# Attention with routed experts on one core: the value products of a head pair in one run, both heads of a step in one operation, and the slot table behind the first expert tile

## The chip, the cores and the metric

One core of a Trainium2 chip runs the whole program. The metric is the device time of one launch in microseconds. The change is read from the median of several launches; the profile is of one launch.

## What is computed

The reference is causal attention with a decay, a routed layer with eight experts, and a dense layer with a rational activation. Cut to what matters here (4 batches, 8 heads, 576 positions, head size 64; all float32):

```python
scores = q @ k.T / 8 + (cum_i - cum_j)          # cum: running sum of log f
attn = softmax(where(j > i, -1e9, scores))      # rows of 576
x = (attn @ v) as 2304 rows of 512
e = argmax(x @ w_gate)                          # one of 8 experts a row
y = gate * sigmoid * (relu(x @ w1[e]) @ w2[e])  # 512 -> 1024 -> 512
h = y @ w_in                                    # 512 -> 2048
g = (a0 + a1 h + a2 h^2 + a3 h^3) / (1 + |b0||h| + |b1| h^2 + 1e-6)
out = g @ w_out                                 # 2048 -> 512
```

## The kernel before

**Attention.** The loop `pair(p)` takes two heads at a time, 16 pairs for 4 batches. A pair has seven steps: a step is a query tile of 128 rows of one head (i = 0 to 3), the last 64 rows of both heads together (i = 4, "tail"), or, for i = 1 and i = 0, the same tile of both heads as two sets of operations. In a step TensorE makes the scores (`scores`, L444 and L445, two products that together keep float32 accuracy), VectorE adds the mask and finds the row minimum of the negated scores (`least`, L466), ScalarE takes the exponential and the row sum (`weights`, L496), TensorE transposes the weights by blocks of 128 keys (`t2`, L587; `t0` and `t1`, L564 and L568, for the tail), and VectorE or ScalarE copies the transposes from PSUM to the tile pT (`move`, helper lines L280 and L282). Then `pv` (L614) multiplies pT with the values: queries 256 to 575 of both heads are one part, queries 0 to 255 the other. Head 0 fills output rows 0 to 63 and head 1 rows 64 to 127, so these products have the tile shape 128*64 in the profile, where scores and transposes have 128*128. A part is a sum over key blocks j; each j is an operation of its own, and the last block has 64 keys, which makes its shape 64*64. Behind each part an `evac` copies the sum (`ot`). After four pairs `batch(b)` makes the router's logits and the expert choice.

What runs next to what is not in the code's order. Each operation is recorded in a `Plan` with the engines that may take it, their assumed lengths, what it needs, which buffers it takes and frees, and a wished time `when`. `Plan.order` simulates the engines; among operations that could start within NEAR ns of the first it takes the one with the smallest `when`. It decides which engine copies what, too. The wished times are T0 = p * 10000 plus the offsets in the T_ table. PSUM has three banks for scores, three for transposes, two for value products.

**Routing tail.** Behind the last pair, VectorE turns the choices into a table `ids`: which token rows stand in which of 25 slots of 128 rows, each slot of one expert. Then 15 small operations (L1016 to L1030) make `esl`: for each slot whether its expert is new, and the next expert.

**Expert stage.** Weights are split into a high and a low half, `wu[u]` for u = 0 to 3 (two of w1, two of w2). `split_unit(u)` does it in two pieces: ScalarE the high halves, VectorE or GpSimd the low ones (L1060). GpSimd gathers the rows of a slot (`gather`, L1142), TensorE transposes them (`trans_x`, L1161), ScalarE and VectorE make colAh and colAl of them (L1086, L1087), `mm1` (L1167 to L1169) multiplies with w1, `trans_h` (L1182) transposes the result, `mm2` multiplies with w2 into py. In between run `pieces`: the decoding of w_in and w_out for the dense layer, on VectorE, ScalarE and GpSimd's DMA queue. `slot_tokens` and `dense_rows` prepare the dense layer's addresses; `spill` is a flag for rare extra slots. In this stage every engine's order is the code's order.

**Dense stage.** `layer1` and `layer2` over 18 token tiles of 128 rows in five groups (L1374 to L1376, L1419 to L1421).

Of the kernel before, what the change touches and what calls it, by code (L numbers as in the profile page):

```python
# [21 lines left out]
P = 128  # L22
# [15 lines left out]
DEAR = {"ACT": 55.11, "DVE": 322.316}  # L38

NEAR = 106.68  # L40

WARM = 6830


class Op:
    def __init__(self, when, lengths, emit, needs, takes, frees):
        self.when, self.lengths, self.emit = when, lengths, emit
        self.needs, self.takes, self.frees = needs, takes, frees
        self.engine = self.start = self.end = None
# [6 lines left out]
class Plan:  # L56
# [5 lines left out]
    def op(self, when, lengths, emit, needs=(), takes=(), frees=()):  # L62


        o = Op(when, lengths, emit, [n for n in needs if n], list(takes), list(frees))
        self.ops.append(o)
        return o
# [5 lines left out]
    def order(self):  # L73
# [5 lines left out]
        waits = {o: len(o.needs) for o in self.ops}  # L79
        users = {}  # L80
# [5 lines left out]
        def start(o, e):  # L86
            t = max([free.get(e, 0)] + [n.reaches(e) for n in o.needs])
# [8 lines left out]
        while ready:  # L96
# [18 lines left out]
            if e == "PE" and t < WARM:  # L115
                n *= 2
            o.engine, o.start, o.end = e, t, t + n
# [14 lines left out]
def tile_attention_moe_mlp(  # L132
# [81 lines left out]
    with ExitStack() as actx, ExitStack() as rctx:  # L214
# [23 lines left out]

        mask = wk.tile([P, NQ * P], F32, name="mask", bufs=1)
# [14 lines left out]
        NS = len(steps)  # L254

        SPAN = 10000
        T_TRANS = (0.627, 0.134, 0.472, 0.384, 0.239, 0.344, 0.231)
        T_MOVE = (0.739, 0.791, 0.043, -0.438, 0.442, 0.349, 0.365)
        T_LEAST, T_EXP, T_SPLIT, T_SPLIT2 = -0.021, -0.001, 0.692, 0.56
        T_PV, T_PV2, T_PVJ, T_OUT = 1.505, 0.222, 0.046, 0.218  # L260
        T_BATCH, T_BATCHJ, T_ROWS = 0.768, 0.136, 1.212
# [22 lines left out]
        def evac_len(n):  # L284
            return {"ACT": 50 + 0.836 * n, "DVE": 65 + 1.04 * n}
# [64 lines left out]
        def pair(p):  # L350
# [18 lines left out]
            def load_v(e):  # L369
                d["v"] = lt("v", (P, 2, NI, D))  # L370
                nc.sync.dma_start(out=d["v"][:, :, 0:NQ, :], in_=v4[b, hp])
                nc.sync.dma_start(out=d["v"][0:TL, :, NQ, :], in_=vt[b, hp])
# [7 lines left out]
            for h0, h1 in one:  # L380
                n = 820 * (h1 - h0) if p else 1300
# [5 lines left out]
            l_v = plan.op(tl + 0.5 * SPAN, {"SP": 900}, load_v, takes=["v"])  # L387
# [35 lines left out]
            for h in range(2):  # L423
                w = ts + h * T_SPLIT2 * SPAN
                o_kh.append(plan.op(w, {"DVE": 369}, kh(h), [lk[h]] + o_kh[:1], takes=["kh"] if h == 0 else []))
                o_qh.append(plan.op(w + 1, {"ACT": 573}, qh(h), [lq[h]] + o_qh[:1], takes=["q"] if h == 0 else []))
                kle = {"POOL": 1450} if p else {"DVE": 669}
                qle = {"POOL": 1450} if p else {"DVE": 669}
                q2e = {"POOL": 1000} if p else {"DVE": 400}
# [8 lines left out]
            def scores(h, i, u):  # L438
                def go(e):
                    c0 = i * P if h == 0 else S + P + TL + i * P  # L440
                    n = max((i + 1) * P, 256)
                    u["ps"] = bank(ps_s, "s")
                    lhs = d["q"][:, c0 : c0 + P]
                    nc.tensor.matmul(u["ps"][:, :n], lhs, d["kh"][:, h, :n], start=True, stop=False)  # L444
                    nc.tensor.matmul(u["ps"][:, :n], d["q2"][:, c0 : c0 + P], kl_[:, h, :n], start=False, stop=True)  # L445
# [15 lines left out]
            def least(h, i, u):  # L461
                def go(e):
                    w = (i + 1) * P
                    u["t"] = wt("t")
                    u["mn"] = wk.tile([P, 2], F32, tag="mn", name="mn", bufs=8)
                    nc.vector.tensor_tensor_reduce(  # L466
                        out=u["t"][:, :w], in0=u["ps"][:, :w], in1=mask[:, NQ * P - w :], scale=SCALE, scalar=3.0e38,
                        op0=ALU.add, op1=ALU.min, accum_out=u["mn"][:, 0:1],
                    )
# [21 lines left out]
            def weights(h, i, u):  # L491
                def go(e):
# [3 lines left out]
                    nc.scalar.activation(  # L496
# [28 lines left out]
            for si, step in enumerate(steps):  # L525
# [3 lines left out]
                for h, i in step:  # L529
# [9 lines left out]
                    else:  # L539
                        prev, first_e = None, None  # L540
                        oss = []
                        for c in (0, hw):
# [3 lines left out]
                            if c == 0:  # L546
                                first_l = prev
# [958 lines left out]
```

## Time and profile before

| | us |
|---|---|
| time, median of 3 launches (lowest, highest) | 952.83 (952.47, 953.22) |
| time of the profiled launch | 949.95 |
| its span, first to last instruction | 948.1 |
| TensorE busy | 894.9 (94%) |
| VectorE busy | 755.4 (80%) |
| ScalarE busy | 623.7 (66%) |
| GpSimd busy | 347.2 (37%) |

Busy times are of the profiled launch. TensorE's products overlap and their ends are modelled, so how long a product holds the engine is read from the start of it to the start of the next one, not from its own duration.

### The profile page before, as it was taken

What the parts mean: (1) busy time and instruction counts of PE and PEld (TensorE: products, weight loads), DVE (VectorE), ACT (ScalarE), POOL (GpSimd) and SP (SyncE); (2) the same over time, 40 slices, a digit from 0 to 9 for tenths busy, and PEclk for the clock granted to TensorE, in tenths of its full rate; (3) what the DMA queues carried; (4) which work ended last, traced back from release to release, by engine and by line L of the source; (5) the groups of instructions that cost most, each with busy time, mean ns of one, the idle gap of its engine ahead of it and who ended that gap; (6) DMA issues with size and microseconds to landing.
All of it is one profiled execution on the core that took longest, in us unless ns stands there. A gap on an engine that the chain in (4) does not pass through costs nothing. (4 is left out here: it accounts for less than half of the span.)

```text
span 948.1 us, 14923 instructions
## 1 busy us (share of the span) xinstructions
PE 894.9 (94%) x4732; PEld 713.5 (75%) x4733; DVE 755.4 (80%) x1410; ACT 623.7 (66%) x1274; POOL 347.2 (37%) x357
## 2 busy tenths in 40 slices
PE   5999999995589999999999999999999999999996
PEld 5665666563368888888888778889988889988885
DVE  6778888877948668978785499989989878889873
ACT  3787777777036456756653487887777677777664
POOL 7766565624612221312331123243332324223223
PEclk8999999998789999999999999999999999999999
DMA  6754546702455537878864312100100001000001
GB/s 171 168 150 131 157 127 207 210 15 99 138 208 189 194 114 273 298 257 285 287 228 145 135 57 67 34 27 30 34 34 12 23 1 45 24 1 34 1 0 45
DMA packets 50148, 110.26 MB, mean 116 GB/s; under 512 B 8405, under 2 KB 12526, under 8 KB 50062
## 3 DMA queue, kind: packets, MB, share of 16 engines
q1 hardware_dynamic: 39214, 74.09, 25.6%
q0 software_dynamic: 10848, 35.14, 10.8%
q8 instruction: 39, 0.64, 0.3%
q14 instruction: 47, 0.39, 0.1%
HBM read 151.79 MB, written 20.35 MB: 182 GB/s over the span
## 5 line engine op out<-in xcount | busy, mean ns | idle before, releaser
L1405 POOL TENSOR_TENSOR gl<-raw,gh 128x512 fp32r<-128x512 f32 (+1 forms) x80 | 95.4, 1194 | 243.4 <-ACT gh L1404 151.1
L1421 PE MATMUL pa<-wu,gl 128*128 128x512 f32 x288 | 113.0, 392 | 1.1 <-POOL gl L1405 1.1
L1419 PE MATMUL pa<-wu,gh 128*128 128x512 f32 x288 | 113.7, 395 | 0.0
L1420 PE MATMUL pa<-wu,gh 128*128 128x512 f32 x288 | 112.6, 391 | 0.0
L1384 ACT ACTIVATE raw<-ph 128x512 f32<-128x512 f32 (+1 forms) x80 | 44.3, 553 | 79.9 <-PE ph L1376 76.7
L496 ACT ACTIVATE pr<-t,mn 128x384 f32<-128x384 f32 (+3 forms) x128 | 71.1, 557 | 27.6 <-DVE mn L466 25.8
L1087 DVE TENSOR_TENSOR colAl<-px,colAh 128x512 fp32r<-128x512 f32 x70 | 48.0, 687 | 51.4 <-ACTq L1098 28.4
L1060 DVE TENSOR_TENSOR wu<-raw,wu 128x1024 fp32r<-128x1024 f32 x60 | 81.0, 1391 | 7.5 <-ACT wu L1058 7.3
L1387 DVE SCALAR_TENSOR_TENSOR raw<-raw,babs 128x512 f32<-128x512 f32 (+1 forms) x80 | 60.8, 760 | 24.2 <-ACT raw L1385 23.9
L1397 DVE SCALAR_TENSOR_TENSOR raw<-raw,coef,raw 128x512 f32<-128x512 f32 (+1 forms) x80 | 65.9, 824 | 17.6 <-ACT raw L1393 14.5
L1168 PE MATMUL ph<-wu,colAh 128*128 128x512 f32 x176 | 70.7, 402 | 8.2 <-DVE wu L1060 8.2
L1374 PE MATMUL ph<-colAh,wi 128*128 128x512 f32 x192 | 74.9, 390 | 0.8 <-ACTq L1315 0.8
L1375 PE MATMUL ph<-colAl,wi 128*128 128x512 f32 x192 | 74.8, 390 | 0.2 <-DVEq L1315 0.2
L1167 PE MATMUL ph<-wu,colAh 128*128 128x512 f32 x176 | 74.2, 421 | 0.7 <-ACT colAh L1086 0.7
L1376 PE MATMUL ph<-colAh,wi 128*128 128x512 f32 x192 | 74.7, 389 | 0.0
L466 DVE CUSTOM_DVE_ANT_0 t<-s,mask 128x384 f32<-128x384 f32 (+3 forms) x128 | 60.3, 485 | 16.9 <-ACT ot L280 6.9
L1169 PE MATMUL ph<-wu,colAl 128*128 128x512 f32 x176 | 70.7, 402 | 0.0
L1167 PE MATMUL py<-wu,colAh 128*128 128x512 f32 x176 | 70.5, 400 | 0.0
L1169 PE MATMUL py<-wu,colAl 128*128 128x512 f32 x176 | 68.8, 391 | 0.0
L1168 PE MATMUL py<-wu,colAh 128*128 128x512 f32 x176 | 68.7, 390 | 0.0
L614 PE MATMUL po<-pT,v 128*64 128x320 f32 (+4 forms) x448 | 66.4, 380 | 0.4 <-DVE pT L282 0.4
L1086 ACT ACTIVATE colAh<-px 128x512 fp32r<-128x512 f32 x70 | 41.6, 596 | 38.2 <-PE px L1182 25.2
(236 smaller groups left out, 2456.4 us busy)
## 6 DMA issues: line engine op xcount, KB each, us to landing
raw<-in_w_dram SPq DMA_DIRECT2D x92, 1024.0 KB
rk<-in_kT_dram SPq DMA_DIRECT2D x30, 288.0 KB
rq<-in_qT_dram SPq DMA_DIRECT2D x30, 288.0 KB
d<-in_w_in_dram POOLq DMA_DIRECT2D x16, 512.0 KB
d<-in_w_out_dram POOLq DMA_DIRECT2D x16, 512.0 KB
y_d<-ys SPq DMA_DIRECT2D x22, 256.0 KB
v<-in_v_dram SPq DMA_DIRECT2D x16, 256.0 KB
wo_d<-d SPq DMA_DIRECT2D x16, 256.0 KB
```

The source lines that it names most:

```text
L496: nc.scalar.activation(u["pr"][:, :w], u["t"][:, :w], AF.Exp, bias=u["mn"][:, 0:1], scale=-1.0, accum_out=sm[:, i, 2 * hp + h : 2 * hp + h ...
L1060: on.tensor_tensor(w[:, 1], r, w[:, 0].bitcast(F32), ALU.subtract)
L1167: nc.tensor.matmul(ps, hi[:, c, :], w[:, 0, c, :], start=start and c == 0, stop=False)
L1168: nc.tensor.matmul(ps, hi[:, c, :], w[:, 1, c, :], start=False, stop=False)
L1169: nc.tensor.matmul(ps, lo[:, c, :], w[:, 0, c, :], start=False, stop=stop and c == KD - 1)
L1374: nc.tensor.matmul(out_, wh, hi[:, :, c], start=(c == 0), stop=False)
L1375: nc.tensor.matmul(out_, wh, lo[:, :, c], start=False, stop=False)
L1376: nc.tensor.matmul(out_, wl_, hi[:, :, c], start=False, stop=(c == KD - 1))
L1405: nc.gpsimd.tensor_tensor(d["gl"], d["u_"], d["gh"].bitcast(F32), ALU.subtract)
L1419: nc.tensor.matmul(a_, gh[:, sl], wh, start=(m == 0), stop=False)
L1420: nc.tensor.matmul(a_, gh[:, sl], wl_, start=False, stop=False)
L1421: nc.tensor.matmul(a_, gl[:, sl], wh, start=False, stop=(m == MF - 1))
```

## The change

Seven things are changed.

1. In `pv` all key blocks of a part are one operation of the plan, where each block was one. Nothing of another kind can be put between them. The plan knows a `shape` for TensorE's operations and adds SWITCH = 130 ns when it changes.
2. For i = 1 and i = 0 the scores, row minima, exponentials, transposes and copies of both heads are one operation each: the scores of both share a bank, the copy is one instruction.
3. The last key block of the values is 128 deep. The 64 last keys stand in the lower half of the tile, the upper half is zero (three tiles `vs`, set once), and the tail's transposes take the last 128 columns.
4. The T_ table, DEAR, NEAR and the lengths of some operations have other values; the steps have wished times of their own.
5. The 15 operations for `esl` become `slot_info()`, which is called behind `trans_x(0)`.
6. The low halves of wu[1] are made ahead of `trans_x(0)`, and those of wu[2] and wu[3] by VectorE, where GpSimd did it.
7. The load of the spill flag moves to the end of slot 2, `slot_tokens` stands at slot 1 beside `dense_rows`, and the gathers of the token words begin at slot 3.

The diff, cut:

```diff
-NEAR = 106.68
+NEAR = 108.2
+SWITCH = 130
...
-            t = max([free.get(e, 0)] + [n.reaches(e) for n in o.needs])
+            t = free.get(e, 0) + (SWITCH if e == "PE" and o.shape != shape else 0)
+            t = max([t] + [n.reaches(e) for n in o.needs])
...
+        vs = [ld.tile([P, 2, NI, D], F32, name=f"v{i}", bufs=1) for i in range(3)]
+        for t in vs:
+            nc.gpsimd.memset(t[: P - TL, :, NQ], 0.0)
...
-        T_PV, T_PV2, T_PVJ, T_OUT = 1.505, 0.222, 0.046, 0.218
+        T_PV, T_PV2, T_OUT = -2.976, 4.84, -4.781
...
+                    for m, h in enumerate(hs):
+                        c0 = i * P if h == 0 else S + P + TL + i * P
+                        o = u["ps"][:, m * n : (m + 1) * n]
+                        nc.tensor.matmul(o, d["q"][:, c0 : c0 + P], d["kh"][:, h, :n], start=True, stop=False)
+                        nc.tensor.matmul(o, d["q2"][:, c0 : c0 + P], kl_[:, h, :n], start=False, stop=True)
...
-                        nc.tensor.transpose(x["b"][:TL, :P], u["pr"][:, NQ * P : S], identf)
+                        nc.tensor.transpose(x["b"][:, :P], u["pr"][:, S - P : S], identf)
...
-                def pv(j, x=x, part=part, base=base, end=end, last=last):
-                    def go(e):
-                        if j == 0:
-                            x["po"] = bank(ps_o, "po")
-                        kk = P if j < NQ else TL
+                def pv(e, x=x, base=base, end=end, last=last):
+                    x["po"] = bank(ps_o, "po")
+                    for j in range(last + 1):
                         lo = max(base, j * P)
                         for h in range(2):
                             nc.tensor.matmul(
                                 x["po"][h * D : (h + 1) * D, lo - base : end - base],
-                                d["v"][:kk, h, j, :], d["pT"][:kk, h, j, lo:end],
+                                d["v"][:, h, j, :], d["pT"][:, h, j, lo:end],
                                 start=(j == 0), stop=(j == last),
                             )
...
     for u in range(4):
-        split_unit(u, lo=(u == 0))
+        split_unit(u, lo=False)
...
         for s in range(3):
             gather(s)
+        split_unit(0, hi=False)
+        split_unit(1, hi=False)
         trans_x(0, col_of(0))
+        slot_info()
         weights(0, 0)
-        split_unit(1, hi=False)
         weights(1, 0)
-        spill = nc.values_load(esl[NPIPE : NPIPE + 1, 3 : 4], min_val=0, max_val=1)
...
-                split_unit(2, hi=False, on=nc.gpsimd)
+                split_unit(2, hi=False)
...
-                split_unit(3, hi=False, on=nc.gpsimd)
+                split_unit(3, hi=False)
```

What the plan makes of it is seen in the order of the instructions. First TensorE in the second and third pair, before; `po` is a value product, `s` a score, `pt` a transpose.

```order
L614 MATMUL po<-pT,v 64x320 x2
L587 MATMUL pt<-identf,pr 128x128 x4
L444 MATMUL s<-kh,qs_113 128x384
L445 MATMUL s<-kl_119,q2s_117 128x384
L614 MATMUL po<-pT,v 64x320 x2
L587 MATMUL pt<-identf,pr 128x128 x3
L614 MATMUL po<-pT,v 64x192 x2
L614 MATMUL po<-pT,v 64x64 x2
```

One run of value products is cut into single key blocks by transposes and scores of the next pair. The same products of that pair after the change:

```order
L455 MATMUL s<-kh,qs_113 128x256
L456 MATMUL s<-kl_119,q2s_117 128x256
L616 MATMUL po<-pT,v_130 64x320 x6
L616 MATMUL po<-pT,v_130 64x192 x2
L616 MATMUL po<-pT,v_130 64x64 x2
L616 MATMUL po<-pT,v_130 64x256 x2
L616 MATMUL po<-pT,v_130 64x128 x2
L573 MATMUL pt<-identf,pr 128x128 x4
```

Both parts of the pair now stand together, seven key blocks with two heads each. Up to the last of them, 92 such runs stand in TensorE's order before, and 16 after.

The second place is VectorE behind the routing tail (`esl` and `info` belong to the slot operations, `wu` to the splits, `colAl` to the token tiles). Before:

```order
L1028 TENSOR_SCALAR esl<-en 25x1
L1029 SCALAR_TENSOR_TENSOR esl<-en,chg 25x1
L1030 CAST esl<-usd 25x1
L1060 TENSOR_TENSOR wu_3514<-raw_82,wu_3514 128x1024 x2
L1087 TENSOR_TENSOR colAl<-px,colAh 128x512
L1060 TENSOR_TENSOR wu_3515<-raw_83,wu_3515 128x1024 x2
L1263 TENSOR_LOAD esl
L1087 TENSOR_TENSOR colAl<-px,colAh 128x512
```

After the change, from the ids on:

```order
L1007 TENSOR_SCALAR ids<-pid 128x25
L1037 TENSOR_TENSOR wu_3323<-raw_82,wu_3323 128x1024 x2
L1037 TENSOR_TENSOR wu_3324<-raw_83,wu_3324 128x1024 x2
L1064 TENSOR_TENSOR colAl<-px,colAh 128x512
L1112 TENSOR_SCALAR info<-send_3241,pcol 25x9
```

The splits of wu[0] and wu[1] stand ahead of the first token tile, and the slot operations behind it. Further on in the same order, after the change, the splits that GpSimd made before:

```order
L1209 TENSOR_SCALAR d_3487<-d_3483 128x512
L1211 SCALAR_TENSOR_TENSOR d_3487<-d_3483,d_3487 128x512
L1037 TENSOR_TENSOR wu_3325<-raw_84,wu_3325 128x1024 x2
L1213 SCALAR_TENSOR_TENSOR d_3487<-d_3483,d_3487 128x512
L1216 SCALAR_TENSOR_TENSOR d_3487<-da,d_3487 128x512
L1075 COMPARE_AND_BRANCH
L1037 TENSOR_TENSOR wu_3324<-raw_83,wu_3324 128x1024 x2
L1075 UNCONDITIONAL_BRANCH x2
L1223 TENSOR_TENSOR wi_3327<-d_3487,wi_3327 128x512
L1064 TENSOR_TENSOR colAl<-px,colAh 128x512
L1037 TENSOR_TENSOR wu_3326<-raw_85,wu_3326 128x1024 x2
```

wu[2] and wu[3] (the numbers 3325 and 3326) stand among the decoding steps; the split between the two branches is skipped while the expert stays the same.

## Rows read from the trace of the kernel before

**Rows 1.** Busy time by stretch (us from the span's start), instructions, clock, DMA

```profile
core 0: us, PE busy (x) PEld busy (x) DVE busy (x) ACT busy (x) POOL busy (x), PEclk, DMA share, GB/s
13.49:219.23 205.74, 194.45 (x1344) 128.34 (x1344) 163.69 (x544) 153.49 (x478) 118.49 (x126) 0.99 0.55 146
...
240.04:272.45 32.41, 19.44 (x67) 13.20 (x66) 23.22 (x31) 5.20 (x10) 15.99 (x12) 0.72 0.55 187
272.45:948.10 675.65, 665.96 (x3163) 559.87 (x3161) 542.05 (x775) 446.97 (x760) 190.56 (x180) 1.00 0.31 104
```

**Rows 2.** Timeline of TensorE in attention: start, us, engine, line, operation

```profile
130.40 0.66 PE L587 MATMUL pt<-identf,pr 128*128 128x128 f32 x4
130.98 0.76 PE L614 MATMUL po<-pT,v 128*64 128x320 f32 x4
131.67 0.44 PE L444 MATMUL s<-kh,qs 128*128 128x384 f32 x1
...
132.22 0.76 PE L614 MATMUL po<-pT,v 128*64 128x320 f32 x4
...
133.39 0.81 PE L614 MATMUL po<-pT,v 128*64 128x192 f32 x8
134.12 0.39 PE L444 MATMUL s<-kh,qs 128*128 128x256 f32 x1
```

**Rows 3.** Timeline of TensorE in the first pairs

```profile
28.42 1.30 PE L614 MATMUL po<-pT,v 128*64 128x320 f32 x8
29.65 0.40 PE L455 MATMUL s<-kh,qs 128*128 128x288 f32 x1
...
31.71 0.34 PE L444 MATMUL s<-kh,qs 128*128 128x384 f32 x1
...
32.06 0.49 PE L587 MATMUL pt<-identf,pr 128*128 128x128 f32 x3
```

**Rows 4.** Timeline of TensorE, transposes in a row in the last pair

```profile
214.16 1.04 PE L587 MATMUL pt<-identf,pr 128*128 128x128 f32 x8
215.03 0.60 PE L779 MATMUL pt<-identf,ot 128*128 128x128 f32 x4
```

**Rows 5.** Timeline of VectorE at the expert stage's start; idle before in brackets

```profile
240.15 0.21 DVE L1016 TENSOR_SCALAR eq<-send,pcol 25x9 f32<-25x9 f32 x1
...
242.13 2.34 DVE L1060 TENSOR_TENSOR wu<-raw,wu 128x1024 fp32r<-128x1024 f32 x2
245.42 0.69 DVE L1087 TENSOR_TENSOR colAl<-px,colAh 128x512 fp32r<-128x512 f32 x1 [0.95 <-ACT colAh L1086]
246.03 12.63 DVE L1060 TENSOR_TENSOR wu<-raw,wu 128x1024 fp32r<-128x1024 f32 x2
```

**Rows 6.** Timeline of GpSimd in the same stretch

```profile
241.91 0.97 POOL L1142 DMA_INDIRECT xg<-x_d,ids  x1 [0.30 <-issue]
...
247.11 9.32 POOL L1060 TENSOR_TENSOR wu<-raw,wu 128x1024 fp32r<-128x1024 f32 x4
```

**Rows 7.** Timeline of TensorE there

```profile
257.58 0.80 PE L1168 MATMUL ph<-wu,colAh 128*128 128x512 f32 x1 [8.16 <-DVE wu L1060]
...
266.44 0.38 PE L1132 MATMUL px<-identf,ids_t 128*25 128x128 f32 x1 [3.90 <-DVE ids_t L1130]
...
272.45 0.48 PE L1167 MATMUL py<-wu,colAh 128*128 128x512 f32 x1
```

**Rows 8.** Busy time in four us there, columns as in rows 1

```profile
256.00:260.00 4.00, 2.42 (x6) 1.93 (x7) 3.82 (x5) 0.00 (x0) 0.44 (x1) 0.50 0.11 9
```

**Rows 9.** VectorE's copies in attention by shape: count, busy us, mean ns, idle before

```profile
L282 DVE COPY pT<-pt 128x512 f32<-128x512 f32 x14 | 9.4, 674 | 4.2 <-PE pt L587 4.2
...
L282 DVE COPY pT<-pt 128x128 f32<-128x128 f32 x16 | 4.3, 280 | 0.0
...
L282 DVE COPY pT<-pt 128x256 f32<-128x256 f32 x7 | 2.7, 395 | 0.4 <-PE pt L587 0.4
```

**Rows 10.** Timeline of ScalarE at the first block of w_in

```profile
252.51 0.66 ACT L1206 ACTIVATE da<-d 128x512 f32<-128x512 f32 x1 [2.64 <-DMA d<-in_w_in_dram]
```

**Rows 11.** TensorE's waits in attention: total us, times, longest us

```profile
PE s L444 <- DVE mn L466: 4.4, 6, 1.1
```

More of the change, by code (lines that the diff above doesn't have):

```diff
@@ L34, with __init__ @@
 }
-DEAR = {"ACT": 55.11, "DVE": 322.316}
-NEAR = 106.68
+DEAR = {"ACT": 45.9, "DVE": 316.0}
+NEAR = 108.2
 WARM = 6830
+SWITCH = 130
 class Op:
-    def __init__(self, when, lengths, emit, needs, takes, frees):
-        self.when, self.lengths, self.emit = when, lengths, emit
+    def __init__(self, when, lengths, emit, needs, takes, frees, shape):
+        self.when, self.lengths, self.emit, self.shape = when, lengths, emit, shape
         self.needs, self.takes, self.frees = needs, takes, frees
@@ L60, in __init__, with op @@
         self.buffers, self.ops = buffers, []
-    def op(self, when, lengths, emit, needs=(), takes=(), frees=()):
-        o = Op(when, lengths, emit, [n for n in needs if n], list(takes), list(frees))
+    def op(self, when, lengths, emit, needs=(), takes=(), frees=(), shape=0):
+        o = Op(when, lengths, emit, [n for n in needs if n], list(takes), list(frees), shape)
         self.ops.append(o)
@@ L79, in order @@
         waits = {o: len(o.needs) for o in self.ops}
+        shape = 0
         users = {}
@@ L116, in order @@
                 n *= 2
+            if e == "PE":
+                shape = o.shape
             o.engine, o.start, o.end = e, t, t + n
@@ L615, in go @@
                                 x["po"][h * D : (h + 1) * D, lo - base : end - base],
-                                d["v"][:kk, h, j, :], d["pT"][:kk, h, j, lo:end],
+                                d["v"][:, h, j, :], d["pT"][:, h, j, lo:end],
                                 start=(j == 0), stop=(j == last),
                             )
-                    return go
-                prev = first = None
-                for j in range(last + 1):
-                    lo = max(base, j * P)
-                    prev = plan.op(wP + dP * j, {"PE": (end - lo) * 4 / 2.4 + 58}, pv(j), (o_pv_need[part] if j == 0 else []) + [prev, l_v],
-                                   takes=[] if j else ["po"], frees=[("pT", pt_first[0]), ("v", l_v)] if j == last else [])
-                    first = first or prev
+                n_cols = sum(end - max(base, j * P) for j in range(last + 1))
+                first = prev = plan.op(
+                    wP, {"PE": n_cols * 4 / 2.4}, pv, o_pv_need[part] + [l_v], takes=["po"],
+                    frees=[("pT", pt_first[0]), ("v", l_v)], shape=1,
+                )
                 def out_t(e, x=x, base=base, end=end):
```

199 lines of the change are left out of this document (95 added, 104 removed).

## The prediction

> **What bounds the kernel now.** I read the busy times by stretch first [rows 1]. Three of the stages matter: attention (13.49 to 219.23 us), the start of the expert stage (240.04 to 272.45, behind the routing tail), and the rest. In attention TensorE is busy 194.45 of 205.74 us, 94.5%; VectorE 163.69 (80%), ScalarE 153.49 (75%). So TensorE is the bound, and VectorE is not far behind. In the expert start nothing is full: TensorE 19.44 and VectorE 23.22 of 32.41 us. From 272.45 on TensorE is full, 665.96 of 675.65. So time saved ahead of 272.45 moves the end by as much, unless a new wait appears behind it.
>
> Next, how TensorE fills attention. Its timeline shows the products with the values (L614, 64 output columns a head, so shape 128*64) as single key blocks between transposes and scores (128*128) [rows 2]. A lone 320-column block holds the engine from 130.98 to 131.67, 0.69 us. Two blocks in a row take 1.23 us (28.42 to 29.65) [rows 3], so a block is worth 1.23 - 0.69 = 0.54, and 0.15 is lost in each run. The neighbours lose as well: four transposes between two such runs take 0.58 (130.40 to 130.98) against 4 x 0.109 = 0.44 (eight take 0.87, 214.16 to 215.03 [rows 4]); a pair of 384-column scores takes 0.55 (131.67 to 132.22) against 0.35 (31.71 to 32.06 [rows 3]). So one run costs 0.15 + 0.14 = 0.29 beside transposes and 0.15 + 0.20 = 0.35 beside scores.
>
> Then the expert start. The VectorE timeline has the slot operations from 240.15 to 242.13, then the low halves of wu[0], two pieces in 2.34 us, so 1.17 each, then those of wu[1], two pieces in 12.63 us [rows 5]. In those microseconds GpSimd ran its four pieces for wu[2] and wu[3], 247.11 to 256.43 [rows 6]: VectorE's second piece came out only after GpSimd was through. TensorE sat 8.16 us for it, sat 3.90 us more for the token ids queued on VectorE, and began mm2 of slot 0 at 272.45 [rows 7]; behind the first wait it came back at the lower clock, 1.2 GHz (0.50 granted [rows 8]).
>
> **The change part by part.** *Runs of the value products.* Counted in the order of TensorE's instructions, 92 runs become 16: one per pair, both parts together. 76 runs at 0.29 to 0.35, middle 0.32, are 24.3 us. In addition the 64-row block of the last keys becomes 128 rows deep: today its run (192 and 64 columns, 133.39 to 134.12 [rows 2]) takes 0.73, where 256 columns at 0.54 / 320 are 0.43 and the run loses 0.15, so 0.15 is left for this inner change of shape; 16 times, 2.4. The extra 64 key rows cost nothing: the column count is the same, and the zeros are set once by three small memsets, under the loads that the first scores wait for. TensorE's need falls by 26.7, to 167.8 us.
>
> *Both heads in one operation.* Per pair two 256-column and two 128-column copies become one of 512 and one of 256. On VectorE that is 2 x 395 + 2 x 280 = 1350 ns against 674 + 395 = 1069 [rows 9]; 16 pairs give 4.5 us, and I take ScalarE's price for the same. By the counts in the order the new table takes 19 copies off VectorE (92 become 73) and 13 off ScalarE (116 become 103), wide ones and narrow ones exchanged, so the most comes off VectorE: about 4 and 1. Needs: VectorE 159.5, ScalarE 152.5.
>
> *What attention then takes.* TensorE at today's 94.5% would need 177.5 us: 28 saved. The other end: VectorE at today's 80% needs 200 us: 5 saved. Between them I take TensorE at 90%, 186 us, VectorE at 86%: **20 saved**. It is nearer the first end since TensorE still needs most. What speaks for a loss of share is the run of 3 us itself (1600 columns at 0.54 / 320, plus its edges), in which no score and no transpose is made. VectorE then lives on at most three score banks, some 1.6 us at the price of like-sized copies (0.40 to 0.67 [rows 9]), and on the transposes waiting. It may starve for 1 us a pair; with 186 us it has (186 - 159.5) / 16 = 1.7 us a pair to spare, so this is covered, barely.
>
> *Expert start.* The two pieces for wu[1] go ahead of the first colAl, those for wu[2] and wu[3] leave GpSimd, and the slot operations stand behind colAl. VectorE: ids at 240.15, four pieces of 1.17 until 244.8, still ahead of colAl at 245.42, which waits for ScalarE [rows 5]. So mm1 of slot 0 starts as now. The slot operations then take 2.0 until 248.1; they delay only the weight loads on SP, whose targets are wanted some 20 us later. The half product mm1(0,1) runs on at 257.58 - 8.16 = 249.4. The next that is late is mm2(0,0), which needs the transposed h of slot 0. By the new VectorE order, each step at the price of colAl's 0.69 if it is as wide: second colAl until about 250.7, two decode steps at most 1.4, wu[2] 2.34, two decode steps 1.4, about 0.9 for ScalarE's answer, 0.69 for wi, 0.69 for colAl: 258.1. TensorE has the rest of mm1(0,1), mm1(1,0) and three sets of four transposes to do, 35 instructions at the 0.21 us that one takes in the full stretch (665.96 / 3163 [rows 1]): 7.4, until 256.8. So it waits over 1 us there. 272.45 - 258.1 = 14.3 saved, if the first w_in block has landed by 250.7. Now ScalarE waited for it until 252.51 [rows 10], behind weight loads that will start later; if it is no earlier, 12.5. **I take 14.** The spill flag's register load, formerly ahead of mm1(0,0) on every engine, moves to slot 2; I cost it at nothing, since TensorE waited for colAh there. Token ids and dense rows, now together at slot 1, are some 1.5 us of VectorE in a stage where TensorE is the bound. The routing tail keeps its operations: 0, give or take 1.
>
> The sum: -20 - 14 = -34 against this execution's 949.95 us (span 948.1 and 1.85 around it), 916. The median of the runs shown is 2.9 above it, so the time as measured should be **919 us**.
>
> **A page beside the rows.** The Trainium skill, "TensorEngine Tiling (Array Packing)", PSUM Bottleneck, says that tiling makes TensorE faster but not the copies out of PSUM, which may then become the limit. By it the copies, VectorE's above all, would set attention, and the time would be that of rival 1. No run here shows it yet.
>
> **The rivals.** *1. VectorE or the bursts set attention.* VectorE gets no busier than today's 80%: 5 saved there, 14 at the expert start: 934 us. For it: VectorE at 159.5 and TensorE at 167.8 are near each other, and the runs of 3 us. Against it: VectorE idles 42 us now, with a TensorE that is full. 0.20.
>
> *2. The first gathers are held.* GpSimd issues them as soon as the ids are there, now while VectorE runs four split pieces. If GpSimd has to let all pass, 4 x 1.17 = 4.7 us are lost: 924 us. Against it: the gather at 241.91 took 0.97 [rows 6], with VectorE's pieces from 242.13 on [rows 5]. 0.07. The Trainium skill, "SBUF — State Buffer", SBUF: two separate sides, gives VectorE and GpSimd a port pair that one of them holds for its whole instruction, and warns that descriptor writing on GpSimd can be locked out by it. The trace shows the lock between operations with two inputs on both engines (the 12.63 us), and not with this gather.
>
> *3. TensorE keeps its 94.5%.* 28 + 14 saved: 911 us. 0.07.
>
> *4. Slower.* A whole run waits for its last copy from PSUM, and all later scores and transposes of TensorE stand behind it; before, single blocks slipped between. TensorE at 90% already idles 186 - 167.8 = 18 us, 1.1 a pair; it decides from 34 / 16 = 2.1 us a pair more, 3.2 in all. Against it: TensorE's waits on VectorE's row minima come to 4.4 us in attention, the longest 1.1 [rows 11], and in the new order scores of another pair mostly stand between a pair's last transposes and its run. 0.03, about 960 us.
>
> *5. The attention part gives nothing* (the new order loses what the runs save): 14 alone, 939 us. 0.03.
>
> **How the numbers follow.** The forecast has 0.60, its own range 912 to 926 (attention 15 to 25, expert start 11 to 15). The range that holds 8 in 10 reaches over rivals 2 and 3 and most of rival 1: 907 to 935. A measurement of this kernel can tell 0.2%, 1.9 us, from no change. Rival 4 ends slower; in 0.02 I expect the sum to come to nothing. That is 0.95 faster, 0.02 the same, 0.03 slower.
>
> **What would show it.** Right: the value products in 16 runs of about 3 us; attention at 181 to 191 us with TensorE busy near 168; pieces of 1.2 us for all of wu on VectorE, no wait of 8.16 us, a granted clock of 1.00 from the first mm1 on, mm2 of slot 0 some 18 us after the ids. Wrong: TensorE waits of over 1.5 us a pair for copies into pT or row minima (rival 1 or 4), a first gathered tile transposed later than 4 us after the ids (rival 2), or new waits of TensorE behind the expert start.

## Result and the profile after

The changed kernel takes **915.87 us** (median of 4 runs, 915.42 to 916.76) against 952.65 for the kernel before in the same session: ratio 0.9617, 95% interval 0.9601 to 0.9634. The profiled execution took 916.76 us, its span 915.0 (before 949.95 and 948.1).

The stretches of the kernel after, with TensorE (PE), its weight loads, VectorE (DVE), ScalarE (ACT) and GpSimd (POOL) busy in us, the granted clock, the share of the DMA engines and GB/s. They answer to [rows 1] and [rows 8]:

```profile
core 0: us, PE busy (x) PEld busy (x) DVE busy (x) ACT busy (x) POOL busy (x), PEclk, DMA share, GB/s
13.52:192.90 179.38, 167.24 (x1340) 135.94 (x1340) 155.53 (x525) 148.00 (x464) 118.56 (x127) 0.98 0.62 167
192.90:214.00 21.10, 8.63 (x87) 6.41 (x87) 17.08 (x48) 14.50 (x23) 10.87 (x11) 0.79 0.32 113
214.00:232.05 18.05, 15.50 (x66) 9.95 (x65) 13.20 (x28) 4.14 (x8) 8.05 (x8) 0.86 0.69 231
214.00:915.00 701.00, 685.18 (x3227) 570.63 (x3225) 560.02 (x810) 452.43 (x768) 197.78 (x188) 0.99 0.32 109
246.00:250.00 4.00, 4.00 (x13) 3.05 (x13) 0.88 (x4) 0.09 (x1) 0.00 (x0) 0.57 0.41 137
```

Attention fell from 205.74 to 179.38 us, the routing tail went from 20.81 to 21.10, and the part from the ids to the end fell from 708.06 to 701.00: -26.4 + 0.3 - 7.1 = -33.2, the spans' difference of 33.1.

TensorE's timeline after (start, time, line and operation, in brackets the idle time before and what ended it), answering to [rows 2, 7]:

```profile
189.95 3.02 PE L616 MATMUL po<-pT,v 128*64 128x320 f32 x28
218.83 0.66 PE L1163 MATMUL px<-identf,xg 128*128 128x128 f32 x4 [0.60 <-DMA xg<-x_d,ids]
232.05 0.50 PE L1169 MATMUL py<-wu,colAh 128*128 128x512 f32 x1 [1.27 <-ACT colAh L1063]
245.26 0.27 PE L1134 MATMUL px<-identf,ids_t 128*25 128x128 f32 x1 [3.21 <-DVE ids_t L1132]
250.07 0.48 PE L1169 MATMUL py<-wu,colAh 128*128 128x512 f32 x1
```

The 28 products of a pair are now one run of 3.02 us. In the expert stage mm2(s,k) is half k (0 or 1) of slot s's product with w2. mm2(0,0) starts 18.05 us behind the ids (32.41 before), with no wait of 8 us ahead of it. But slot 1 stops for the transposed token ids, 3.21 us, and the products behind that wait run at a granted clock of 0.57, so mm2(1,0) stands 250.07 - 214.00 = 36.07 us behind the ids. Before it was 284.76 - 240.04 = 44.72:

```profile
284.76 0.48 PE L1167 MATMUL py<-wu,colAh 128*128 128x512 f32 x1
```

VectorE and GpSimd there, answering to [rows 5] and [rows 6]:

```profile
214.00 0.19 DVE L1007 TENSOR_SCALAR ids<-pid 128x25 int32<-128x25 f32 x1 [0.40 <-PE pid L1005]
214.31 4.63 DVE L1037 TENSOR_TENSOR wu<-raw,wu 128x1024 fp32r<-128x1024 f32 x4
220.77 0.38 DVE L1112 TENSOR_SCALAR info<-send,pcol 25x9 f32<-25x9 f32 x1
244.33 0.69 DVE L1216 SCALAR_TENSOR_TENSOR d<-da,d 128x512 f32<-128x512 f32 x1
244.94 0.17 DVE L1132 CAST ids_t<-ids 128x25 f32<-128x25 int32 x1
```

```profile
214.48 2.00 POOL L1144 DMA_INDIRECT xg<-x_d,ids  x1 [4.70 <-DVE ids L1007]
216.79 1.86 POOL L1144 DMA_INDIRECT xg<-x_d,ids  x1 [0.31 <-issue]
218.96 0.95 POOL L1144 DMA_INDIRECT xg<-x_d,ids  x1 [0.30 <-DMA xg<-x_d,ids]
```

Four low halves take 4.63 us, 1.16 each. The cast of the ids is a 0.17 us step that stands behind VectorE's whole list for the slot. The first two gathers, beside the four pieces, took about twice the 0.97 of [rows 6] and the 1.08 of the first one before:

```profile
240.52 1.08 POOL L1142 DMA_INDIRECT xg<-x_d,ids  x1 [4.70 <-DVE eq L1016]
```

TensorE's waits from 40 to 190 us (us in all, times, longest), to be set beside [rows 11]:

```profile
PE s L466 <- DVE mn L478: 4.8, 2, 2.6
PE pt L713 <- ACT lgs L705: 1.4, 1, 1.4
PE pt L593 <- DVE pT L292: 0.7, 1, 0.7
```

### The profile page after: what moved, and what is told of

It reads as the page before. It is cut to its first block, busy times and chain, and to the rows that moved or that the text cites. A ratio compares the mean times of both kernels' runs of the same rounds, so it can differ in the third digit from the quotient of the medians.

```text
span 915.0 us, 14857 instructions
## 1 busy us (share of the span) xinstructions
PE 868.4 (95%) x4733; PEld 720.1 (79%) x4733; DVE 742.2 (81%) x1395; ACT 619.1 (68%) x1261; POOL 339.6 (37%) x356
## 3 DMA queue, kind: packets, MB, share of 16 engines
q1 hardware_dynamic: 39214, 74.09, 26.4%
q0 software_dynamic: 10848, 35.14, 11.3%
## 5 line engine op out<-in xcount | busy, mean ns | idle before, releaser
L1037 DVE TENSOR_TENSOR wu<-raw,wu 128x1024 fp32r<-128x1024 f32 x64 | 75.4, 1221 | 8.4 <-ACT wu L1035 8.0
L510 ACT ACTIVATE pr<-t,mn 128x384 f32<-128x384 f32 (+3 forms) x128 | 70.6, 555 | 16.1 <-DVE mn L478 15.6
L1401 DVE SCALAR_TENSOR_TENSOR raw<-raw,coef,raw 128x512 f32<-128x512 f32 (+1 forms) x80 | 66.0, 825 | 17.4 <-ACT raw L1397 14.4
L1063 ACT ACTIVATE colAh<-px 128x512 fp32r<-128x512 f32 x70 | 41.6, 596 | 37.4 <-PE px L1184 26.1
L1035 ACT ACTIVATE wu<-raw 128x1024 fp32r<-128x1024 f32 x64 | 63.8, 1053 | 3.2 <-DMA raw<-in_w_dram 2.8
L1425 PEld LDWEIGHTS pa<-wu,gl 128*128 128x128 f32 x288 | 54.0, 188 | 14.0 <-POOL gl L1409 2.4
```

Source lines behind the costliest of these rows:

```text
L510: nc.scalar.activation(u["pr"][:, sl], u["t"][:, sl], AF.Exp, bias=u["mn"][:, m : m + 1], scale=-1.0, accum_out=sm[:, i, 2 * hp + h : 2 * ...
L1037: nc.vector.tensor_tensor(w[:, 1], r, w[:, 0].bitcast(F32), ALU.subtract)
L1425: nc.tensor.matmul(a_, gl[:, sl], wh, start=False, stop=(m == MF - 1))
```

## The experiments

My theory had two parts. In attention, TensorE loses time each time it changes the shape of its matmuls, so grouping gains what the changes cost. In the expert start, GpSimd's splits held VectorE up (below: the lock), and that wait is gone. The rivals: the gain of attention comes from the merged heads and new due times (the wished times of the plan); the expert start is worth nothing, or hangs on the order of VectorE's list rather than on GpSimd. All ratios are to the kernel before; the change stands at 0.9617.

How much one profiled execution can tell: five kernels with the change's attention took 179.38 to 181.51 us in it, five with the old one 205.74 to 210.11. From the ids to the end, kernels that differ only in attention from the change took 700.38 to 702.16.

### Attention: one part undone, or one part alone

**The products apart.** The changed kernel with one planned operation for each key block again, and a rule that keeps like shapes apart:

```diff
-            t = free.get(e, 0) + (SWITCH if e == "PE" and o.shape != shape else 0)
+            t = free.get(e, 0) + (200 if e == "PE" and o.shape == shape == 1 else 0)
...
-                first = prev = plan.op(
-                    wP, {"PE": n_cols * 4 / 2.4}, pv, o_pv_need[part] + [l_v], takes=["po"],
+                for j in range(last + 1):
+                    n_cols = end - max(base, j * P)
+                    prev = plan.op(wP, {"PE": n_cols * 4 / 2.4}, pv(j), ...
```

> This is the changed kernel in which a query part's value products are one planned operation for each key block again, and the plan is told to keep same-shaped operations apart: the products stand in 103 runs between other shapes instead of 16; the heads stay merged and the expert start stays as changed. My theory, that entering and leaving the value products' tile shape costs TensorE time (0.29 to 0.35 us for a run): 87 more runs by 0.32 are 28 us more of TensorE, and the attention is 20 to 28 us longer than the 179.4 us of the change, total 935 to 944 us. Rival: the attention's gain came from the merged heads' fewer copies and the new table of due times; then this kernel is within 5 us of the change (915 to 921 us).

Measured: 947.82 us, ratio 0.9949 (0.9932 to 0.9965), above the theory's 935 to 944. Its attention:

```profile
13.56:225.20 211.64, 200.68 (x1348) 133.72 (x1350) 159.14 (x527) 150.37 (x462) 120.49 (x130) 0.98 0.53 142
```

32.3 us longer than in the change, TensorE's busy time 33.4 more: 0.37 to 0.38 us for each of 87 runs, a little over the price that I took, and attention is more than the expected 20 to 28 us longer. The rival falls: merged heads and new due times without the grouping are not faster in attention than the kernel before. The due times were made for grouped products, though, so this run doesn't show what merged heads are worth with a table made for products apart.

**The last key block over 64 rows again.**

```diff
+                        kk = P if j < NQ else TL
-                                d["v"][:, h, j, :], d["pT"][:, h, j, lo:end],
+                                d["v"][:kk, h, j, :], d["pT"][:kk, h, j, lo:end],
...
-                        nc.tensor.transpose(x["b"][:, :P], u["pr"][:, S - P : S], identf)
+                        nc.tensor.transpose(x["b"][:TL, :P], u["pr"][:, NQ * P : S], identf)
```

> This is the changed kernel with the last key block's value products over 64 rows as before, not 128 rows with zeros in half of them. The prediction priced the shape change inside a run at 0.15 us for each of the 16 products of that block, 2.4 us of TensorE. By the prediction: 2 to 3 us slower than the change (918 to 919 us), with TensorE's busy time in the attention 2.4 us up. Rival: in the trace of the change a step from another shape costs only as much as the shape behind it makes it, and the last product of a run leaves for scores or transposes in either case: within 0.7 us of the change (915.2 to 916.6 us).

Measured: 922.18 us, ratio 0.9681 (0.9655 to 0.9708). Attention and one run:

```profile
13.41:197.76 184.35, 173.36 (x1341) 137.13 (x1341) 154.74 (x525) 148.72 (x464) 118.87 (x126) 0.97 0.62 162
...
194.51 3.32 PE L617 MATMUL po<-pT,v 128*64 128x320 f32 x28
```

Neither number: attention is 5.0 us longer and TensorE 6.1 us busier, where the prediction had 2.4. One run shows why for most of it: 3.32 against 3.02 us, 0.30 for each of 16 runs, 4.8 in all. The 64-column block stands inside the run, ahead of the 256-column block of the second part, so its shape is entered and left; the prediction had counted 0.15. The 1.3 us of busy time that are left are not the block's for certain: behind a wait of 1.96 us for row minima this trace has a short stretch at half clock (granted 0.50, so 1.2 GHz), in which the same products take longer. The trace of the change has none in attention after 40 us, though it waits 2.21 us at the same place; the products apart and the merged products alone have one too, near 101 us.

```profile
103.00:106.00 3.00, 3.00 (x17) 3.00 (x15) 2.10 (x8) 2.46 (x8) 1.20 (x2) 0.50 0.03 5
```

**The heads apart.** The changed kernel with every (head, block) a step of its own, the due times of a pair written twice:

```diff
-        steps = [[(0, 2)], [(0, 3)], [(0, NQ)], [(1, 3)], [(1, 2)], [(0, 1), (1, 1)], [(0, 0), (1, 0)]]
+        steps = [[(0, 2)], [(0, 3)], [(0, NQ)], [(1, 3)], [(1, 2)], [(0, 1)], [(1, 1)], [(0, 0)], [(1, 0)]]
```

> This is the changed kernel with the steps of the two heads as operations of their own again, each with the due time that the pair had: the value products stand in 32 runs instead of 16, and the small copies of the first two query blocks are twice as many. My theory: 16 more runs by 0.32 us are 5 us more of TensorE, the copies 4 to 5 us more of VectorE and ScalarE together, so 4 to 8 us more than the change (920 to 924 us). Rival A (VectorE is close behind TensorE and now sets the end): 8 us or more (924 and up). Rival B (only the value products' grouping counts, and runs of the small parts are hidden): under 2 us more (916 to 918 us).

Measured: 933.58 us, ratio 0.9801 (0.9768 to 0.9835), by its profile 14.7 us more in attention and tail together. Rival A's number, but not its reason:

```profile
13.54:211.49 197.95, 182.83 (x1377) 143.57 (x1377) 157.79 (x524) 159.37 (x513) 123.18 (x132) 0.98 0.59 156
211.49:228.74 17.25, 4.90 (x49) 3.21 (x49) 14.11 (x39) 10.97 (x16) 5.74 (x6) 0.68 0.25 83
...
PE pt L593 <- DVE pT L292: 4.2, 2, 2.2
```

VectorE is at 80% there and ScalarE at 81%, TensorE at 92%; TensorE's own busy time rose most, by 15.6 us, of which 16 more runs at 0.32 explain 5. What makes up the rest isn't shown; the next run bears on it.

**The products merged, nothing else**, on the kernel before with its own due times:

```diff
-                    prev = plan.op(wP + dP * j, {"PE": (end - lo) * 4 / 2.4 + 58}, pv(j), (o_pv_need[part] if j == 0 else []) + [prev, l_v],
+                first = prev = plan.op(
+                    wP, {"PE": n_cols * 4 / 2.4 + 58}, pv, o_pv_need[part] + [l_v], takes=["po"],
```

> This is the kernel before with its value products merged into one planned operation for each query part, and nothing else changed (heads apart, the last key block over 64 rows, the old expert start and the old due times): 32 runs instead of 92. By the price of 0.29 to 0.35 us for a run, 60 runs are 19 us of TensorE; at the share that TensorE then held the attention goes from 205.7 to 186 to 191 us, the time is 14 to 20 us under before (933 to 939 us). Rival (from the run with the heads apart, which was 16 us slower than the change): the grouping alone starves VectorE and ScalarE, and without merged heads and fitted due times only 5 to 10 us are saved (943 to 948 us).

Measured: 938.56 us, ratio 0.9865 (0.9846 to 0.9885), 13.1 us under before in the same session. The time is inside the theory's 933 to 939 us and the saving just short of its 14 to 20; attention, at 193.04, is above its 186 to 191. The rival's 5 to 10 us fall.

```profile
13.61:206.65 193.04, 180.37 (x1362) 137.10 (x1362) 153.12 (x534) 154.94 (x492) 120.19 (x127) 0.98 0.60 156
206.65:225.16 18.51, 6.48 (x64) 4.60 (x64) 17.07 (x49) 12.62 (x19) 8.68 (x9) 0.69 0.33 115
...
PE pt L587 <- DVE pT L282: 6.3, 3, 3.0
```

The kernel before has this wait for copies too, in the same window of 40 to 190 us:

```profile
PE pt L587 <- DVE pT L282: 3.2, 2, 1.6
```

Attention and tail together are 211.55 us here, 226.55 before, 200.48 in the change, 215.20 with the heads apart. So grouping alone, at 32 runs, gives 15.0 of the 26.1 us, with 3.1 us more of waits for copies; merged heads, the 128-row block and the new table give the other 11.1, and some 4.8 of these are the block (above). The kernel with the heads apart has this grouping and the block, and is still 3.7 us slower than grouping alone. So something else in it costs time, and its 14.7 us are no price of the heads; the table of due times, made for merged heads, is the likeliest, but no run shows it. Merged heads and table can't be told apart by these runs.

One count goes with most of this. I went through TensorE's records in attention and counted where a matmul has other row or column counts than the one ahead of it: 231 changes before, 44 in the change, 99, 140 and 222 in the kernels with 64 rows, with merged products alone and with products apart. Busy time above the change's, divided by the changes more: 27.2 / 187 = 0.146, 6.1 / 55 = 0.11, 13.1 / 96 = 0.14, 33.4 / 178 = 0.19 us for each. With the heads apart the count fails: 85 changes, 15.6 / 41 = 0.38, or 11.9 / 34 = 0.35 with the tail, of which this kernel does 3.7 us of TensorE's work earlier. So changes of shape are not all that makes TensorE busier there, and the price of one is known only as a range.

### The expert start

Eight kernels run here change it. The table gives, from each trace, the us from the start of the ids on VectorE to mm2(0,0), to mm2(1,0), and to the end of the span.

| kernel | mm2(0,0) | mm2(1,0) | end |
|---|---|---|---|
| before | 32.41 | 44.72 | 708.06 |
| before, low halves on VectorE | 28.59 | 40.92 | 704.58 |
| before, tokens at slot 1 | 25.94 | 43.24 | 707.47 |
| before, both of these | 18.50 | 37.27 | 701.41 |
| before, the whole new start | 18.80 | 37.59 | 701.93 |
| after | 18.05 | 36.07 | 701.00 |
| after, two low halves on GpSimd | 25.47 | 44.04 | 709.12 |
| after, gathers first | 18.54 | 36.36 | 701.72 |
| after, ids early | 17.72 | 30.69 | 696.01 |
| after, ids early and gathers first | 18.00 | 32.38 | 697.68 |

**The new start on the kernel before**, the attention as it was (the hunks from `slot_info` on, as in the diff of the change):

> This is the kernel before with the expert-start part of the change alone (all four low halves on VectorE, gathers issued earlier, the facts of the slots worked out later); the attention stays as it was, with its 92 runs of value products. My theory from the trace of the change: mm2(0,0) comes about 14 us nearer to the token ids, but the wait for the transposed ids (3.2 us) and the lower clock behind it give some 5.7 us back before slot 1, and the later slots about 1 more, so that 7 to 9 us of the time before are saved (944 to 946 us) and mm2(1,0) comes 8.7 us nearer to the ids. Rival A: the start is worth its full 14 us when the attention in front of it is unchanged (939 us). Rival B: the start is worth nothing, and all 37 us come from the attention (952 us).

Measured: 945.66 us, ratio 0.993 (0.9904 to 0.9957), 4 to 9 us saved. The time and mm2(0,0), 13.6 us nearer to the ids, are as the theory had them. mm2(1,0) came 7.1 us nearer for an expected 8.7, and ids to end gained 6.1 us for an expected 7 to 9. Both rivals are out.

**Only the low halves moved to VectorE:**

```diff
-                split_unit(2, hi=False, on=nc.gpsimd)
+                split_unit(2, hi=False)
...
-                split_unit(3, hi=False, on=nc.gpsimd)
+                split_unit(3, hi=False)
```

> This is the kernel before with one thing changed: the low halves of the third and fourth expert unit are subtracted on VectorE instead of GpSimd, in the same places of the program. My theory (GpSimd's split and VectorE's held each other up in the kernel before): VectorE's pieces there fall from 12.63 to about 2.4 us, TensorE's wait of 8.16 us in front of mm2(0,0) is gone, and most of the 14 us that the start gained in the change are seen already, so 5 to 10 us less than before (943 to 948 us). Rival: the wait is one for VectorE's place in line, not for the shared port; the four GpSimd pieces then only move to VectorE, and the time is within 2 us of before (951 to 955 us).

Measured: 948.23 us, ratio 0.995 (0.9932 to 0.9968): 3 to 6.5 us saved, 3.5 from ids to end, at or under the low end of the theory's 5 to 10. The rival's time is out, but what it says of VectorE's line holds in part: the lock is gone, and the wait is not.

```profile
254.33 2.35 DVE L1060 TENSOR_TENSOR wu<-raw,wu 128x1024 fp32r<-128x1024 f32 x2
260.05 2.35 DVE L1060 TENSOR_TENSOR wu<-raw,wu 128x1024 fp32r<-128x1024 f32 x2
263.38 0.17 DVE L1130 CAST ids_t<-ids 128x25 f32<-128x25 int32 x1
...
263.70 0.38 PE L1132 MATMUL px<-identf,ids_t 128*25 128x128 f32 x1 [11.31 <-DVE ids_t L1130]
```

Every piece takes 1.2 us now. Before, the piece that the lock held was the first of wu[1]'s two, not the second, as the prediction reads it:

```profile
246.03 11.50 DVE L1060 TENSOR_TENSOR wu<-raw,wu 128x1024 fp32r<-128x1024 f32 x1
```

In this run TensorE sits 11.31 us for a 0.17 us cast that is queued on VectorE behind these pieces and the decode steps.

**Only the token ids moved, from slot 0 to slot 1:**

```diff
-            if s == 0:
-                slot_tokens()
             if s == 1:
+                slot_tokens()
                 dense_rows()
```

> This is the kernel before with the cast and transpose of the token ids moved from slot 0 to slot 1, and nothing else changed; GpSimd still splits two units. By the prediction the 8.16 us wait stays and only the 3.90 us wait for the ids leaves the front of mm2(0,0): mm2(0,0) about 28 us after the ids instead of 32.4, the time 1 to 4 us under before (949 to 952 us). Rival: the place of the token ids in VectorE's line is what sets mm2(0,0), and the splits on GpSimd only fill the wait: mm2(0,0) at 18 to 22 us, 8 us or more under before.

Measured: 950.61 us, ratio 0.9992 (0.9973 to 1.001), no change that can be told. mm2(0,0) came 6.5 us earlier, between the theory's 28 us and the rival's 18 to 22, and mm2(1,0) 1.5: the wait had only moved one slot on.

```profile
257.62 0.80 PE L1168 MATMUL ph<-wu,colAh 128*128 128x512 f32 x1 [8.18 <-DVE wu L1060]
265.97 0.47 PE L1167 MATMUL py<-wu,colAh 128*128 128x512 f32 x1
278.51 0.38 PE L1132 MATMUL px<-identf,ids_t 128*25 128x128 f32 x1 [3.21 <-DVE ids_t L1130]
```

**Both of these moves:**

> This is the kernel before with two things changed at once: the low halves of the third and fourth unit on VectorE, and the token ids moved to slot 1. Alone the first brought mm2(0,0) from 32.4 to 28.6 us after the ids, with an 11.31 us wait for the token ids in front. If these two are the whole of the expert start: mm2(0,0) at 18 to 20 us and the time 6 to 9 us under before (944 to 947 us), as in the run with all of the start's changes. Rival: the earlier split of the second unit and the later slot facts matter as well: mm2(0,0) at 22 us or later, under 5 us saved (above 948 us).

Measured: 946.09 us, ratio 0.9934 (0.9915 to 0.9953). mm2(0,0) at 18.50 us: these two edits are the whole expert start. Alone they brought 3.8 and 6.5 us at mm2(0,0), together 13.9. The earlier second split and the later slot facts add nothing that is seen (18.80 us with the whole new start).

**The two low halves back on GpSimd**, in the changed kernel:

```diff
-                split_unit(2, hi=False)
+                split_unit(2, hi=False, on=nc.gpsimd)
...
-                split_unit(3, hi=False)
+                split_unit(3, hi=False, on=nc.gpsimd)
```

> This is the changed kernel with the low halves of the third and fourth unit back on GpSimd, as before the change; all else as changed. By the prediction (VectorE's and GpSimd's two-input operations hold each other up): VectorE's operations between 220 and 232 us (colAl, the decode steps) grow, mm2(0,0) comes 3 to 8 us later after the ids than the 18.05 us of the change, and the time is 3 to 8 us over the change (919 to 924 us). Rival: what VectorE runs there now, behind the split of the second unit, doesn't collide, and the split is off its queue: mm2(0,0) within 1 us of 18 us or earlier, the time within 1.5 us of the change.

Measured: 925.19 us, ratio 0.9709 (0.9686 to 0.9732), 8.8 us over the change by the ratios, 8.1 by the table, so a little above the theory's 3 to 8. mm2(0,0) came 7.4 us later, and the rival falls. The lock is back, in another place than I had named. GpSimd, VectorE, TensorE:

```profile
223.85 9.37 POOL L1037 TENSOR_TENSOR wu<-raw,wu 128x1024 fp32r<-128x1024 f32 x4
...
222.32 10.93 DVE L1112 TENSOR_SCALAR info<-send,pcol 25x9 f32<-25x9 f32 x1
...
235.91 0.80 PE L1169 MATMUL ph<-wu,colAh 128*128 128x512 f32 x1 [5.86 <-ACTq L1075]
```

The same operation on 25 x 9 numbers takes 0.38 us in the change. Here it came out at 233.25, when GpSimd's pieces ended (233.22), and all of VectorE stood behind it. It had begun 1.5 us ahead of the pieces' first record; what held it in that time isn't shown.

### What the change left behind

**The token ids early:** cast ahead of the first split, transposed behind the first gathered rows at slot 0.

```diff
+        slot_cast()
         split_unit(0, hi=False)
...
+                if s == 0:
+                    slot_tokens()
...
             if s == 1:
-                slot_tokens()
                 dense_rows()
```

> This is the changed kernel with the token ids cast before the first split and transposed behind the first rows at slot 0, not at slot 1 behind VectorE's work. My theory: the 3.21 us that TensorE waits for the cast ids and the lower clock of the products behind it (granted 0.57 in that stretch) are what the start gives back, so mm2(1,0) comes about 5 us nearer to the ids and the time is 4 to 5.5 us under the change (910.4 to 911.9 us). Rival A: the wait moves to VectorE's next late piece (the copies and splits behind), 0 to 1.5 us gained (914.4 to 916). Rival B: the clock falls at this place whatever is waited for: only the wait itself is gained, 3 us (912.5 to 913).

Measured: 912.59 us, ratio **0.9568** (0.9544 to 0.9593), faster than the change with intervals that don't touch, by 4.7 us by the ratios. The median itself is where rival B had it (912.5 to 913), but its reason is out, since the clock didn't fall. From ids to end 5.0 us less, and mm2(1,0) 5.4 us nearer, as the theory had it; its profiled attention was 2.1 us longer, within the spread above. The ids wait for nothing, and the stretch that ran at 0.57 has the full clock:

```profile
225.35 0.27 PE L1139 MATMUL px<-identf,ids_t 128*25 128x128 f32 x1
246.98 0.48 PE L1174 MATMUL py<-wu,colAh 128*128 128x512 f32 x1
...
246.00:250.00 4.00, 4.00 (x22) 3.25 (x21) 3.55 (x9) 3.15 (x5) 2.13 (x3) 1.00 0.54 172
```

**The gathers first:** slot facts, first split, first tile, second split.

```diff
+        slot_info()
         split_unit(0, hi=False)
-        split_unit(1, hi=False)
         trans_x(0, col_of(0))
-        slot_info()
+        split_unit(1, hi=False)
```

> This is the changed kernel with the second unit's low half and the facts of the slots exchanged around the first gathered tile (facts, first split, first tile, second split). My theory: the first gathers took 2.0 and 1.9 us because VectorE's split ran beside their issue; the first split still does, so at most the later tile gains, and the second split now stands behind the first tile's own split on VectorE: within 1 us of the change (915 to 916.5 us). Rival: the gathers fall to about 1.0 us and the first tile is transposed 0.8 us earlier, and all of it reaches the end: 1 to 2 us faster (914 to 915 us).

Measured: 917.52 us, ratio 0.963 (0.9606 to 0.9654), the change's time within the intervals, though the median is 1 us above the expected range. The gathers are short again and the first tile is transposed 4.03 us behind the ids instead of 4.83, but mm2(0,0) is no earlier:

```profile
214.46 1.07 POOL L1144 DMA_INDIRECT xg<-x_d,ids  x1 [4.70 <-DVE info L1112]
217.11 1.05 POOL L1144 DMA_INDIRECT xg<-x_d,ids  x1 [0.30 <-issue]
...
226.49 0.43 DVE L1209 TENSOR_SCALAR d<-d 128x512 uint32<-128x512 uint32 x1 [2.05 <-DMA d<-in_w_in_dram]
...
232.52 0.50 PE L1169 MATMUL py<-wu,colAh 128*128 128x512 f32 x1 [2.65 <-ACT colAh L1063]
```

VectorE waits 2.05 us for the w_in block, which lands no earlier, and mm2(0,0) hangs on what follows from it. The change waits 0.70 us for that block (below). The rival falls.

**Both edits:**

> The two last kernels' edits together. If both are independent: the sum of their gains, 4 to 6.5 us under the change (909.5 to 912 us). Rival: the ids stand in the way of the first split, so less than the better of the two alone (above 912 us).

Measured: 913.28 us, ratio 0.9581 (0.9557 to 0.9604), not told apart from the ids alone. That is the rival's number (above 912), but no run shows its reason. The early ids are the best version found.

## Why the prediction was right, and where its steps were not

The time was 915.87, predicted 919; the profiled execution 916.76, the sum 916. That is closer than the steps were, and luck: attention's saving was put 6 us too small and the expert start's 7 us too large, both outside the ranges that the prediction gave them (15 to 25 and 11 to 15), and the two errors cancelled. The two mechanisms, fewer runs and no split on GpSimd, are borne out.

- *Runs of the value products.* TensorE's need of 167.8 us is measured as 167.24. Inside this sum errors cancel, too. The 64-row block was undersized (some 4.8 for 2.4). Restoring the runs cost more than the priced 0.32 (0.37 us each). Removing 60 of them alone gave less: 14.1 us of TensorE's busy time, 0.23 each, and 12.7 us of attention. Merging the heads was put at nothing on TensorE; with the heads apart it is 15.6 us busier, more than the runs explain.
- *"Between them I take TensorE at 90%, 186 us."* This step failed: TensorE held 93.2%, so 26.4 us were saved, not 20. I had feared that a run of 3 us starves VectorE and that TensorE pays for it afterwards. It idled 12.1 us in attention, not 18, little more than the 11.3 before; its named waits from 40 to 190 us come to 8.4, most of it two waits for row minima. VectorE, at 155.53 us for a forecast 159.5, stands at 87%. With heads apart and the old table the fear comes true in a small part (6.3 us of waits for copies, where the kernel before has 3.2).
- *The page on tiling.* By what the Trainium skill, "TensorEngine Tiling (Array Packing)", PSUM Bottleneck, says, that the copies may become the limit, VectorE would have set attention. The trace doesn't bear that out for the whole change: TensorE at 93% still sets it.
- *Expert start, at mm2(0,0).* Right to 0.1 us: 18.05 us behind the ids, forecast 258.1 - 240.04 = 18.06. That it is so close is luck: the first w_in block came 12.0 us behind the ids, not by the assumed 10.7, and the chain of VectorE that the forecast adds up ended with colAl at 18.89. But mm2(0,0) begins with products that need colAh only, and just its third one waits for colAl (rows below). The reason was half the story. Four splits on GpSimd are a real lock, shown both ways, but with the ids left in VectorE's list at slot 0 taking it away gives 3.8 us, not 14.
- *"Token ids and dense rows, now together at slot 1, are some 1.5 us of VectorE in a stage where TensorE is the bound."* This step failed. At slot 1 TensorE was waiting for VectorE's list: 3.21 us, and slower products behind it. 14.4 us at mm2(0,0) were 8.7 at mm2(1,0) and 7.1 at the end, not 14. The forecast of a full clock from the first mm1 on was wrong for the same reason. The early ids give 5.0 us of it back.
- *From mm2(1,0) on* the change takes 664.93 us and before 663.34. Across all kernels run here this stretch took 663.3 to 665.4, with before the shortest, so whether these 1.6 us come from the change or are scatter stays open.
- *Rivals.* 1, 4 and 5 didn't come. 3 nearly came in attention: 26.4 of its 28 us, with TensorE's share at 93.2% for its 94.5%; the forecast had given it 0.07. 2 came in part (two gathers held, the first tile at 4.83 us, past the 4 us that the prediction named as its sign) and cost next to nothing, since VectorE waits for the w_in block behind it.

The rows after the change on which the reading of mm2(0,0) rests, VectorE's and TensorE's:

```profile
226.03 0.43 DVE L1209 TENSOR_SCALAR d<-d 128x512 uint32<-128x512 uint32 x1 [0.70 <-DMA d<-in_w_in_dram]
...
232.21 0.68 DVE L1064 TENSOR_TENSOR colAl<-px,colAh 128x512 fp32r<-128x512 f32 x1
...
232.95 0.50 PE L1171 MATMUL py<-wu,colAl 128*128 128x512 f32 x1 [0.17 <-DVE colAl L1064]
```

## What to carry to other kernels

Where TensorE is the bound, count how often neighbouring matmuls change shape, inside a planned operation too; here each change was worth 0.11 to 0.19 us of its busy time in four comparisons, and a fifth shows that it is not the only cost. Ask of a tiny step on a busy engine's list not what it costs but who waits for it and what stands ahead: a cast of 0.17 us held TensorE for 3 to 11 us, and moving it out of one wait put it into the next until it was issued ahead of them. Two edits that stand behind each other in one queue must be tried together: alone they brought 3.8 and 6.5 us, together 13.9.

## What the hardware showed unexpectedly

- An operation of VectorE on 25 x 9 numbers took 10.93 us, not 0.38, while GpSimd ran four two-input pieces. So the lock doesn't need two large operations. In the kernel before it held one piece of a split for 11.50 us instead of 1.2. The Trainium skill, "SBUF — State Buffer", SBUF: two separate sides, has one of the two engines hold a shared port pair for a whole instruction; the row agrees, and it shows that several of GpSimd's instructions can pass before VectorE's one gets through (four pieces in both traces).
- Indirect gathers were issued in 2.00 and 1.86 us beside VectorE's split, against 1.08 and 0.97, but one beside the same kind of split in another order took 1.05. What decides it wasn't settled.
